# First-group attention and weight casts re-placed, remainder scores in 64x64 tiles

## The chip, the cores and the metric

The kernel runs on one core of one Trainium2 chip. The metric is the device time of one execution in microseconds (us). The engines are named as in the profile: PE is TensorE (matmuls; its weight loads are listed apart as PEld), DVE is VectorE, ACT is ScalarE, POOL is GpSimd, and SP is SyncE, which here only issues transfers. Each engine runs its own instructions strictly in the order in which they stand in its program, and waits at an instruction until what that one needs is there.

## The reference

Attention with pooled keys and values, followed by a two-layer network with a tanh GELU. In short:

```
k_p = k.reshape(8, 8, 72, 8, 64).mean(axis=3)      # 576 keys become 72, by means of 8
v_p = v.reshape(8, 8, 72, 8, 64).mean(axis=3)
attn = softmax(q @ k_p^T / 8) ; a = attn @ v_p     # per batch and head, q is 8 x 8 x 576 x 64
x = a.transpose(0, 2, 1, 3).reshape(4608, 512)
out = gelu_tanh(x @ w_in) @ w_out                  # w_in 512 x 2048, w_out 2048 x 512
```

Everything comes and goes in float32. The kernel computes with bfloat16 operands in the matmuls.

## The kernel before

The 4608 rows are worked in nine groups of 512 rows. A group g < 8 holds the first 512 query rows of batch g; group 8, called R, holds the remaining 64 rows of all eight batches. The order is 0 to 6, then R, then 7.

For a group the attention of four blocks j of 128 queries is computed: `scores` (queries times pooled keys, into PSUM), `exps` (exponential on ACT), `norm` (row sums and reciprocal on DVE, then the product, written to the tile `eb`, on DVE or POOL), a transpose of `eb` to `eT`, and `values` (into `xT`). `pool` adds up keys and values on DVE, `k_spread` places the pooled keys block-diagonally in `kbd`, and `spread_v` the pooled values in `vbd` with a mask, on POOL. The two-layer part is `hidden` (one of 16 pieces fo of the hidden layer: 4 matmuls against `w_in_b`, then GELU on ACT into `gT`) and `output` (16 matmuls a block against `w_out_b`).

The order of every engine's work is written out by hand: calls stand in program order, and what belongs to the next group is hung into the matmuls of the present one. A hook number s is a place in that stream: `hook(s)` runs just before matmul s, and `at(hooks, s, f, ...)` hangs f there. In the first group (`mlp_first`) the hidden layer goes in chunks of four pieces and in two halves of 256 rows, so that the first half can begin before the attention of query blocks 2 and 3 is finished; hooks 0 to 127 are its 128 matmuls of 256 columns, and hooks from 128 on are the output's matmuls of 512 columns.

SP issues the loads in order. `w_in` arrives in four pieces of 1 MB (`w_in_s`, float32) and `w_out` in four (`w_out_s`); each piece is cast to bfloat16 (`cast_w_in`, `cast_w_out`) by an engine that the call names. The float32 landing tiles share three buffers with the k and v tiles (tag "kv"), so the first load of `w_out` waits for the casts of `w_in` pieces 0 and 1, and its third for those of pieces 2 and 3. PSUM tiles come from two sets: "mm" with four buffers, "sc" with two.

Before the change, `w_in` pieces 0, 1 and 3 are cast on DVE and piece 2 on POOL; the normalization of block 2 of the first group is on POOL, that of block 3 on DVE; both are done before the first hook. The group R computes its scores with 128x64 tiles of the PE array: for each pair of heads one matmul per half of 64 query rows, with 144 columns of keys (two heads side by side, block-diagonal, so that half of the products are with zeros).

Of the kernel before, what the change touches and what calls it, by code (L numbers as in the profile page):

```python
# [10 lines left out]
ALU = mybir.AluOpType  # L11
# [8 lines left out]
def kernel(  # L20
# [21 lines left out]
    nc = tc.nc  # L42
    B, H, S, D = q.shape
    Sp = S // 8
# [5 lines left out]
    HP = H // 2  # L50
    W = H * Sp
# [12 lines left out]
    kbd = consts.tile([128, B, HP, 2, Sp], BF16, name="kbd")  # L64
# [5 lines left out]
    eb = consts.tile([128, 4, 5 * 128], BF16, name="eb")  # L70
# [5 lines left out]
    def copy(eng, out, in_):  # L76
        if eng is nc.scalar:
            eng.copy(out=out, in_=in_)  # L78
        else:
            eng.tensor_copy(out=out, in_=in_)  # L80
# [5 lines left out]
    def rows(t, b):  # L86
        return t[b].rearrange("h (sp pl) d -> (h sp) pl d", pl=8)
# [7 lines left out]
    def load_main(b, which, c0, c1, eng):  # L95
        t, w0, b0 = (k, 0, 0) if which == "k" else (v, 64, 5)
        src = rows(t, b)[w0 + 128 * c0:w0 + 128 * c1].rearrange("(c p) pl d -> p c pl d", p=128)
        eng.dma_start(out=st[b]["kv"][:, b0 + c0:b0 + c1], in_=src)
# [18 lines left out]
    def cast_q(g, j0, j1, eng):  # L117
        if "qb" not in st[g]:
            st[g]["qb"] = work.tile([128, 4, H, D], BF16, name="q_b", bufs=1)
        copy(eng, st[g]["qb"][:, j0:j1], st[g]["q"][:, :, j0:j1].rearrange("p h j d -> p j h d"))  # L120
# [69 lines left out]
    def q_transpose_pe(g, j, eng, tag):  # L190
        tp = psum.tile([128, HP, 128], BF16, name="tp", tag=tag, bufs=BUFS[tag])
        for pr in range(HP):
            nc.tensor.transpose(out=tp[:, pr, :],  # L193
                                in_=st[g]["qb"][:, j, 2 * pr:2 * pr + 2, :].rearrange("p h d -> p (h d)"),
                                identity=identb)
        copy(eng, st[g]["qT"][:, j], tp)
# [5 lines left out]
    def scores(g, j):  # L202
        sc = psum.tile([128, 2, MAIN], F32, name="sc", tag="sc", bufs=2)
        qT = st[g]["qT"]
        for pr in range(HP):
            o = sc[:, pr // 2, 2 * Sp * (pr % 2):2 * Sp * (pr % 2) + 2 * Sp]
            if g < B:
                nc.tensor.matmul(out=o, lhsT=qT[:, j, pr, :], rhs=kbd[:, g, pr].rearrange("d hh s -> d (hh s)"),  # L208
                                 start=True, stop=True)
            else:  # L210
                for half in range(2):
                    p0 = 64 * half
                    nc.tensor.matmul(out=o[p0:p0 + 64], lhsT=qT[:, j, pr, p0:p0 + 64],  # L213
                                     rhs=kbd[:, 2 * j + half, pr].rearrange("d hh s -> d (hh s)"),
                                     start=True, stop=True)
        st[g][("sc", j)] = sc

    def exps(g, j):
        sc = st[g].pop(("sc", j))
        e = work.tile([128, H, Sp], F32, name="e", bufs=4)  # L220
        nc.scalar.activation(out=e.rearrange("p (x h) s -> p x (h s)", x=2), in_=sc[:, :, 0:4 * Sp],  # L221
                             func=ACT.Exp, scale=1.0 / 64.0)
        st[g][("e", j)] = e

    def norm(g, j, eng):
        e = st[g][("e", j)]
        den = work.tile([128, H], F32, name="den")
        nc.vector.reduce_sum(out=den, in_=e, axis=AX.X)  # L228
        r = work.tile([128, H], F32, name="r")
        nc.vector.reciprocal(out=r, in_=den)  # L230
        eng.tensor_tensor(out=eb[:, j, 128 * 5 - W:].rearrange("p (h s) -> p h s", s=Sp), in0=e,  # L231
                          in1=r.unsqueeze(2).to_broadcast([128, H, Sp]), op=ALU.mult)

    def eT_tile(g):
        st[g]["eT"] = work.tile([128, 4, 5, 128], BF16, name="eT", bufs=1)
# [1 line left out]
    def e_transpose_pe(g, j, eng):  # L237
        tp = psum.tile([128, 5, 128], BF16, name="tp", tag="mm", bufs=4)
        for c in range(5):
            nc.tensor.transpose(out=tp[:, c, :], in_=eb[:, j, 128 * c:128 * c + 128], identity=identb)  # L240
        copy(eng, st[g]["eT"][:, j], tp)
# [7 lines left out]
    def values_half(g, half, x, eng):  # L249

        xo = psum.tile([128, 2, 256], F32, name="xo", tag="mm", bufs=4)
        for i in range(2):
            pr = 2 * x + i
            for y, (c, n) in enumerate(PARTS[pr]):
                nc.tensor.matmul(out=xo[:, i, :], lhsT=vbd[:, g, n, :],
                                 rhs=st[g]["eT"][:, 2 * half:2 * half + 2, c, :], start=(y == 0), stop=(y == 1))
        copy(eng, st[g]["xT"][:, 2 * x:2 * x + 2, 256 * half:256 * half + 256], xo)
# [28 lines left out]
    def runner(hooks):  # L286
        def hook(s):
            for f in hooks.pop(s, ()):
                f()
        return hook  # L290
# [44 lines left out]
    def mlp_first(g, hooks):  # L335

        hook = runner(hooks)
        s = 0
        for half, c in [(0, 0), (0, 1), (0, 2), (0, 3), (1, 0), (1, 1), (1, 2), (1, 3)]:
            for fo in range(4 * c, 4 * c + 4):  # L340
                hidden(g, fo, 256 * half, 256 * half + 256, hook, s)
                s += 4
        nc.scalar.preload_act_table_set(EXP_SET)
        o = [psum.tile([128, DM], F32, name="mm", tag="mm", bufs=4) for _ in range(4)]
        for fo in range(12):
            for r in range(4):
                hook(s)
                s += 1
                output(g, r, fo, o[r])
        for r in range(4):  # L350
            for fo in range(12, FO):
                hook(s)
                s += 1
                output(g, r, fo, o[r])
            finish(g, r, o[r], nc.scalar if r == 3 else nc.vector)
        assert not hooks, sorted(hooks)
# [16 lines left out]
    for c in range(2):  # L373
        t = kvp.tile([128, KO, 1024], F32, name="w_in_s", tag="kv")
        w_in_s.append(t)
        for i in range(2):
            nc.sync.dma_start(
                out=t[:, :, 512 * i:512 * i + 512],
                in_=moe_w_in[:, 1024 * c + 512 * i:1024 * c + 512 * i + 512].rearrange("(ko p) f -> p ko f", p=128))

    def cast_w_in(c, eng):
        o = 512 * c
        copy(eng, w_in_b[:, :, o:o + 512], w_in_s[c // 2][:, :, 512 * (c % 2):512 * (c % 2) + 512])
# [3 lines left out]
    def w_out_load(c):  # L387
        if c % 2 == 0:
            w_out_s[c // 2] = kvp.tile([128, 8, DM], F32, name="w_out_s", tag="kv")
        t = w_out_s[c // 2][:, 4 * (c % 2):4 * (c % 2) + 4, :]  # L390
        nc.sync.dma_start(out=t, in_=moe_w_out[512 * c:512 * c + 512, :].rearrange("(fo p) c -> p fo c", p=128))
# [48 lines left out]
    spread_v(0, nc.gpsimd, (0,))  # L440
    pool_v_pe(0, 7, 9, nc.scalar)
    spread_v(0, nc.gpsimd, (1,))
    cast_q(0, 2, 4, nc.gpsimd)
    spread_v(0, nc.gpsimd, (2,))
    warm_up(8, "mm")
    norm(0, 0, nc.vector)
    norm(0, 1, nc.vector)
    e_transpose_pe(0, 0, nc.scalar)
    q_transpose_pe(0, 2, nc.scalar, "mm")
    q_transpose_pe(0, 3, nc.scalar, "mm")  # L450
    e_transpose_pe(0, 1, nc.vector)
    cast_w_in(0, nc.vector)
    scores(0, 2)
    exps(0, 2)
    values_half(0, 0, 0, nc.vector)
    scores(0, 3)
    exps(0, 3)
    values_half(0, 0, 1, nc.scalar)
    nc.scalar.preload_act_table_set(GELU_SET)
    norm(0, 2, nc.gpsimd)  # L460
    cast_w_in(1, nc.vector)
    norm(0, 3, nc.vector)
    cast_w_in(2, nc.gpsimd)

    def first_t(j):
        e_transpose_pe(0, j, nc.vector)

    def first_v():
        cast_w_in(3, nc.vector)
        values_half(0, 1, 0, nc.scalar)  # L470
        values_half(0, 1, 1, nc.vector)

# [4 lines left out]
    load_half(1, "k", nc.sync)  # L477
    load_half(1, "v", nc.sync)
    load_q(1, 0, 4, nc.sync)
    for c in range(4):  # L480
        w_out_load(c)
    load_main(1, "v", 0, 4, nc.sync)

    def load_kv(n):
        if n != B - 1:
# [7 lines left out]
    def at(hooks, s, f, *a):  # L493
        hooks.setdefault(s, []).append(lambda: f(*a))  # L494
# [5 lines left out]
        at(hooks, va, values, n, 1, nc.scalar)  # L500

    hooks = {}
    at(hooks, 16, first_t, 2)
    at(hooks, 32, first_t, 3)
    at(hooks, 42, first_v)
    at(hooks, 66, pool, 1, 0, 4)
    at(hooks, 66, dup_k, 1, 0, 4)
    at(hooks, 66, pool, 1, 4, 5)
    at(hooks, 66, dup_k, 1, 4, 5)
    at(hooks, 80, cast_q, 1, 0, 2, nc.vector)  # L510
    at(hooks, 80, cast_q, 1, 2, 4, nc.vector)
    at(hooks, 96, kT_tile, 1, "sc")
    at(hooks, 96, qT_tile, 1)
    at(hooks, 96, k_transpose_pe, 1, 0, 5)
    at(hooks, 96, k_spread, 1, [nc.vector, nc.vector])
    for j in range(4):
        at(hooks, 104 + 6 * j, q_transpose_pe, 1, j, nc.vector, "sc")
    at(hooks, 122, eT_tile, 1)
    at(hooks, 122, cast_w_out, 0, nc.vector)
    at(hooks, 122, cast_w_out, 1, nc.gpsimd)  # L520
    for j in range(4):
        at(hooks, [126, 127, 136, 140][j], scores, 1, j)
        at(hooks, [128, 128, 136, 140][j], exps, 1, j)
        at(hooks, [136, 140, 144, 148][j], norm, 1, j, nc.vector)
        at(hooks, [136, 140, 144, 148][j], e_transpose_dma, 1, j)
    at(hooks, 141, cast_w_out, 2, nc.scalar)
    at(hooks, 141, cast_w_out, 3, nc.scalar)
    for i in range(2):
        at(hooks, 160, pool, 1, 5 + 2 * i, 7 + 2 * i)
        at(hooks, 160, spread_v, 1, nc.gpsimd, (0, 1) if i == 0 else (2,))  # L530
# [6 lines left out]
    for n_, g in enumerate(seq):  # L537
        if n_ == 0:
            continue
        hooks = {}  # L540
# [69 lines left out]
```

The softmax here doesn't subtract the row's maximum and nothing guards it: scores larger than these inputs give would overflow.

## Time and profile before

| | |
|---|---|
| median of 4 runs | 301.12 us (301.07 to 301.28) |
| profiled execution | 301.1 us |
| its span in the profile | 299.0 us |
| PE busy | 289.1 us (97%) |
| PEld, DVE, ACT, POOL busy | 151.4, 145.9, 158.2, 55.5 us |
| granted TensorE clock | 0.999 |
| transfers | 56.32 MB, mean 188 GB/s |

The share of busy time tells which engine is full: PE. Its idle time lies almost wholly in the first 40 us, where the loads, the casts and the first attention are on the way. Rows of the timeline read: start, duration, engine, line, operation, output<-input, shapes, count of merged instructions, and in brackets the idle time before it with what ended it. Rows of transfers read: target<-source, the engine that issues, count, size, and us from issue to landing. A line number in a row is a line of the kernel before; many operations go through one helper (`copy`, lines 78 and 80), so they are told apart by their tiles.

### The profile page before, as it was taken

How to read it: one execution, taken by the hardware profiler on the slowest of the kernel's cores; microseconds unless marked ns; L12 is line 12 of the kernel's file. 1: busy time of each engine (PE TensorE's matmuls, PEld its weight loads, DVE VectorE, ACT ScalarE, POOL GpSimd, SP SyncE). 2: the span in 40 equal slices, each digit the busy share in tenths (PEclk: the TensorE clock that was granted, in tenths of full speed). 3: DMA queues.
4: the chain of work that ended last, by engine and by line, in shares of the span. 5: the costliest groups of instructions: out<-in, count | busy, mean ns of one | idle time of the engine just before them, and what ended most of it. 6: DMA issues, size and time to landing. Idle time of an engine off the chain costs nothing.

```text
span 299.0 us, 4555 instructions
## 1 busy us (share of the span) xinstructions
PE 289.1 (97%) x1708; PEld 151.4 (51%) x1734; DVE 145.9 (49%) x241; ACT 158.2 (53%) x242; POOL 55.5 (19%) x71
## 2 busy tenths in 40 slices
PE   7869999999999999999999999999999999999996
PEld 7758844445444544454445444544444544444444
DVE  6895769165607570748073807381729100920012
ACT  1487783767157715672577246724773267426500
POOL 3252033230400240024012401240024000100000
PEclk9999999999999999999999999999999999999999
DMA  7999996995699459946994599049944700351012
GB/s 233 355 387 339 384 357 143 348 273 152 135 280 255 134 132 267 275 143 123 260 293 138 122 248 301 2 110 247 277 146 101 164 36 2 79 114 37 0 70 70
DMA packets 73221, 56.32 MB, mean 188 GB/s; under 512 B 45808, under 2 KB 55408, under 8 KB 73200
## 3 DMA queue, kind: packets, MB, share of 16 engines
q1 hardware_dynamic: 73056, 55.98, 68.1%
q8 instruction: 13, 0.21, 0.3%
q10 hardware_dynamic: 144, 0.07, 0.1%
q14 instruction: 8, 0.07, 0.1%
HBM read 36.70 MB, written 9.44 MB: 154 GB/s over the span
## 4 chain that ended last, share of the span: by engine, by line
PE 91%; DVE 3%; DMA 2%; ACT 1%; issue 1%; POOL 1%; SPq 0%; ACTq 0%; POOLq 0%
PE mm L296 40%; PE mm L301 40%; PE xo L266 4%; PE sc L208 2%; DMA kv<-in_k_dram 2%; PE mm L329 1%; DVE den L228 1%; POOL eb L231 1%; PE xo L272 1%; DVE eb L231 1%; PE sc L213 0%; PE tp L193 0%; PE warm L410 0%; ACT gT L298 0%; PE tp L240 0%
## 5 line engine op out<-in xcount | busy, mean ns | idle before, releaser
L296 PE MATMUL mm<-xT,w_in_b 128*128 128x512 bf16 (+1 forms) x632 | 127.3, 357 | 0.9 <-DVE xT L80 0.4
L301 PE MATMUL mm<-w_out_b,gT 128*128 128x512 bf16 x542 | 126.2, 379 | 1.5 <-DVE w_out_b L80 0.5
L298 ACT ACTIVATE gT<-mm 128x512 bf16<-128x512 f32 (+1 forms) x160 | 88.4, 555 | 46.9 <-PE mm L296 45.8
L296 PEld LDWEIGHTS <-w_in_b 128*128 128x128 bf16 x640 | 62.2, 98 | 62.6 <-issue 0.5
L301 PEld LDWEIGHTS <-gT 128*128 128x128 bf16 x560 | 53.4, 98 | 59.7 <-DVE w_out_b L80 0.7
L80 DVE COPY osb<-mm 128x512 f32<-128x512 f32 (+2 forms) x37 | 24.3, 658 | 62.9 <-PE mm L301 58.0
L78 ACT CAST xT<-xo 128x1024 bf16<-128x1024 f32 (+1 forms) x18 | 16.6, 967 | 56.8 <-PE xo L266 49.1
L228 DVE TENSOR_REDUCE den<-e 128x8 f32<-128x576 f32 x36 | 26.5, 737 | 39.8 <-ACT e L221 39.7
L148 POOL TENSOR_TENSOR vbd<-kvb,vmask 128x256 bf16<-128x256 bf16 (+2 forms) x40 | 21.2, 554 | 112.9 <-DVE kvb L130 112.8
L128 DVE TENSOR_TENSOR kv<-kv 128x1024 f32<-128x1024 f32 (+3 forms) x20 | 22.4, 1122 | 28.7 <-DMA kv<-in_v_dram 26.4
L221 ACT ACTIVATE e<-sc 128x576 f32<-128x576 f32 x36 | 22.5, 649 | 9.7 <-ACT e L221 4.0
L231 DVE TENSOR_TENSOR eb<-e,r 128x576 bf16<-128x576 f32 x28 | 26.6, 951 | 1.0
L231 POOL TENSOR_TENSOR eb<-e,r 128x576 bf16<-128x576 f32 x8 | 10.1, 1264 | 72.7 <-ACT e L221 42.3
L80 POOL CAST q_b<-q_sb 128x2048 bf16<-128x2048 f32 (+1 forms) x7 | 15.0, 2146 | 3.4 <-PE mm L301 2.8
L208 PEld LDWEIGHTS <-qT 128*128 128x128 bf16 x128 | 10.1, 98 | 6.9 <-ACT qT L78 0.4
L208 PE MATMUL sc<-kbd,qT 128*128 128x144 bf16 x128 | 13.2, 226 | 0.3 <-ACT qT L78 0.2
L266 PE MATMUL xo<-eT,vbd 128*128 128x512 bf16 x56 | 13.2, 379 | 0.0
L129 DVE TENSOR_TENSOR kv<-kv 128x512 f32<-128x512 f32 (+3 forms) x20 | 12.8, 640 | 0.7
L494 ACT ACT_TABLE_LOAD x8 | 10.3, 1283 | 0.1
L410 PE MATMUL warm<-identb 128*128 128x128 bf16 x112 | 8.9, 246 | 1.4 <-POOL vmask L398 1.4
L80 DVE COPY kbd<-kTd 64x288 bf16<-64x288 bf16 x12 | 5.3, 438 | 8.0 <-DMA kTd<-kvb 7.9
L314 ACT ACT_TABLE_LOAD x7 | 9.0, 1283 | 0.1
(55 smaller groups left out, 99.3 us busy)
## 6 DMA issues: line engine op xcount, KB each, us to landing
out_dram<-osb SPq DMA_DIRECT2D x31, 256.0 KB, 6.5
kv<-in_k_dram SPq DMA_DIRECT2D x7, 1024.0 KB, 6.7
q_sb<-in_q_dram SPq DMA_DIRECT2D x7, 1024.0 KB, 5.8
kv<-in_v_dram SPq DMA_DIRECT2D x7, 1024.0 KB, 9.5
w_in_s<-in_moe_w_in_dram SPq DMA_DIRECT2D x4, 1024.0 KB, 12.6
w_out_s<-in_moe_w_out_dram SPq DMA_DIRECT2D x4, 1024.0 KB, 13.8
out_dram<-osb SPq DMA_DIRECT2D x9, 128.0 KB, 2.3
kv<-in_k_dram SPq DMA_DIRECT2D x2, 512.0 KB, 4.1
```

The lines of the kernel that those rows point to most:

```text
L78: eng.copy(out=out, in_=in_)
L80: eng.tensor_copy(out=out, in_=in_)
L128: add(out=t[:, :, 0:4, :], in0=t[:, :, 0:4, :], in1=t[:, :, 4:8, :], op=ALU.add)
L148: eng.tensor_tensor(out=vbd[p0:128, b, n0:n1, :].rearrange("p (c r) (hh d) -> p c (r hh) d", c=max(m, 1), d=D), in0=kvb[p0:128, 4 + c0:4 + ...
L208: nc.tensor.matmul(out=o, lhsT=qT[:, j, pr, :], rhs=kbd[:, g, pr].rearrange("d hh s -> d (hh s)"), start=True, stop=True)
L221: nc.scalar.activation(out=e.rearrange("p (x h) s -> p x (h s)", x=2), in_=sc[:, :, 0:4 * Sp], func=ACT.Exp, scale=1.0 / 64.0)
L228: nc.vector.reduce_sum(out=den, in_=e, axis=AX.X)
L231: eng.tensor_tensor(out=eb[:, j, 128 * 5 - W:].rearrange("p (h s) -> p h s", s=Sp), in0=e, in1=r.unsqueeze(2).to_broadcast([128, H, Sp]), ...
L266: nc.tensor.matmul(out=xo[:, i, :], lhsT=vbd[:, g, n, :], rhs=eT[:, :, c, :], start=(x == 0), stop=(x == 1))
L296: nc.tensor.matmul(out=hp[:, 0:c1 - c0], lhsT=w_in_b[:, ko, fo * 128:(fo + 1) * 128], rhs=st[g]["xT"][:, ko, c0:c1], start=(ko == 0), stop ...
L298: nc.scalar.activation(out=gT[:, fo, c0:c1], in_=hp[:, 0:c1 - c0], func=ACT.Gelu_apprx_tanh)
L301: nc.tensor.matmul(out=o, lhsT=gT[:, fo, r * 128:(r + 1) * 128], rhs=w_out_b[:, fo, :], start=(fo == 0), stop=(fo == FO - 1))
```

## The change

Four things are changed together.

- In the first group all four `w_in` pieces are cast on POOL, each where it lands; the second half of the q cast goes from POOL to ACT.
- The attention of the first group's query blocks 2 and 3 is re-placed: the values of the first half come before their scores, both xT copies of the first half are on DVE, the normalization of block 2 moves from POOL to DVE and that of block 3 to hook 20, and their transposes and the values of the second half to hooks 20, 33 and 40.
- The chunks of the hidden layer alternate between the halves from the fourth on. Hooks of the second group's preparation move by a few places; `w_out` piece 3 is loaded after v instead of before it, and its cast moves from hook 141 to 156.
- The scores of R are computed in 64x64 tiles, one head of a pair per half of the array's rows: four matmuls of 72 columns for a pair of heads instead of two of 144, without the zeros. The heads therefore stand in another order in `e`, which `norm` undoes when it writes `eb`.

```diff
 def scores(g, j):
         for pr in range(HP):
-            o = sc[:, pr // 2, 2 * Sp * (pr % 2):2 * Sp * (pr % 2) + 2 * Sp]
             if g < B:
+                o = sc[:, pr // 2, 2 * Sp * (pr % 2):2 * Sp * (pr % 2) + 2 * Sp]
...
-            else:
-                for half in range(2):
-                    p0 = 64 * half
-                    nc.tensor.matmul(out=o[p0:p0 + 64], lhsT=qT[:, j, pr, p0:p0 + 64],
-                                     rhs=kbd[:, 2 * j + half, pr].rearrange("d hh s -> d (hh s)"),
-                                     start=True, stop=True)
+                continue
+            for hh in range(2):
+                for p0 in (0, 64):
+                    h0 = 64 * hh
+                    nc.tensor.matmul(out=sc[p0:p0 + 64, hh, Sp * pr:Sp * pr + Sp],
+                                     lhsT=qT[h0:h0 + 64, j, pr, p0:p0 + 64],
+                                     rhs=kbd[h0:h0 + 64, 2 * j + p0 // 64, pr, hh], start=True, stop=True)
 def norm(g, j, eng):
...
+        else:
+            eng.tensor_tensor(out=o.rearrange("p (pr hh s) -> p hh pr s", hh=2, s=Sp),
+                              in0=e.rearrange("p (hh pr) s -> p hh pr s", hh=2),
...
 def mlp_first(g, hooks):
-        for half, c in [(0, 0), (0, 1), (0, 2), (0, 3), (1, 0), (1, 1), (1, 2), (1, 3)]:
+        for half, c in [(0, 0), (0, 1), (0, 2), (1, 0), (0, 3), (1, 1), (1, 2), (1, 3)]:
...
-    cast_q(0, 2, 4, nc.gpsimd)
     spread_v(0, nc.gpsimd, (2,))
     warm_up(8, "mm")
     norm(0, 0, nc.vector)
     norm(0, 1, nc.vector)
+    cast_w_in(0, nc.gpsimd)
+    cast_q(0, 2, 4, nc.scalar)
     e_transpose_pe(0, 0, nc.scalar)
+    e_transpose_pe(0, 1, nc.vector)
     q_transpose_pe(0, 2, nc.scalar, "mm")
     q_transpose_pe(0, 3, nc.scalar, "mm")
-    e_transpose_pe(0, 1, nc.vector)
-    cast_w_in(0, nc.vector)
-    scores(0, 2)
-    exps(0, 2)
     values_half(0, 0, 0, nc.vector)
-    scores(0, 3)
-    exps(0, 3)
-    values_half(0, 0, 1, nc.scalar)
+    values_half(0, 0, 1, nc.vector)
+    for j in range(2, 4):
+        scores(0, j)
+        exps(0, j)
     nc.scalar.preload_act_table_set(GELU_SET)
-    norm(0, 2, nc.gpsimd)
-    cast_w_in(1, nc.vector)
-    norm(0, 3, nc.vector)
+    cast_w_in(1, nc.gpsimd)
+    norm(0, 2, nc.vector)
     cast_w_in(2, nc.gpsimd)
+    cast_w_in(3, nc.gpsimd)
...
     def first_v():
-        cast_w_in(3, nc.vector)
...
-    for c in range(4):
+    for c in range(3):
         w_out_load(c)
     load_main(1, "v", 0, 4, nc.sync)
+    w_out_load(3)
...
-    at(hooks, 16, first_t, 2)
-    at(hooks, 32, first_t, 3)
-    at(hooks, 42, first_v)
+    at(hooks, 20, first_t, 2)
+    at(hooks, 20, norm, 0, 3, nc.vector)
+    at(hooks, 33, first_t, 3)
+    at(hooks, 40, first_v)
...
-    at(hooks, 66, pool, 1, 4, 5)
-    at(hooks, 66, dup_k, 1, 4, 5)
-    at(hooks, 80, cast_q, 1, 0, 2, nc.vector)
-    at(hooks, 80, cast_q, 1, 2, 4, nc.vector)
+    at(hooks, 72, pool, 1, 4, 5)
+    at(hooks, 72, dup_k, 1, 4, 5)
...
+    at(hooks, 100, cast_q, 1, 0, 2, nc.vector)
+    at(hooks, 100, cast_q, 1, 2, 4, nc.vector)
     for j in range(4):
-        at(hooks, 104 + 6 * j, q_transpose_pe, 1, j, nc.vector, "sc")
-    at(hooks, 122, eT_tile, 1)
-    at(hooks, 122, cast_w_out, 0, nc.vector)
-    at(hooks, 122, cast_w_out, 1, nc.gpsimd)
+        at(hooks, 111 + 4 * j, q_transpose_pe, 1, j, nc.vector, "sc")
+    at(hooks, 124, eT_tile, 1)
+    at(hooks, 124, cast_w_out, 0, nc.vector)
+    at(hooks, 124, cast_w_out, 1, nc.gpsimd)
...
-    at(hooks, 141, cast_w_out, 3, nc.scalar)
+    at(hooks, 156, cast_w_out, 3, nc.scalar)
```

More of the change, by code (lines that the diff above doesn't have):

```diff
@@ L230, in norm @@
         nc.vector.reciprocal(out=r, in_=den)
-        eng.tensor_tensor(out=eb[:, j, 128 * 5 - W:].rearrange("p (h s) -> p h s", s=Sp), in0=e,
-                          in1=r.unsqueeze(2).to_broadcast([128, H, Sp]), op=ALU.mult)
+        o = eb[:, j, 128 * 5 - W:]
+        if g < B:
+            eng.tensor_tensor(out=o.rearrange("p (h s) -> p h s", s=Sp), in0=e,
+                              in1=r.unsqueeze(2).to_broadcast([128, H, Sp]), op=ALU.mult)
+        else:
+            eng.tensor_tensor(out=o.rearrange("p (pr hh s) -> p hh pr s", hh=2, s=Sp),
+                              in0=e.rearrange("p (hh pr) s -> p hh pr s", hh=2),
+                              in1=r.rearrange("p (hh pr) -> p hh pr", hh=2).unsqueeze(3).to_broadcast([128, 2, HP, Sp]),
+                              op=ALU.mult)
     def eT_tile(g):
```

## The prediction, made before the changed kernel ran

> **What bounds the kernel now.** I read the page first (span, the ended-last chain), then the timeline of the first 45 us, then single transfers, then the stretch of the remainder's scores. Durations are from the profiled execution, 301.1 us (span 299.0, 2.1 around it); the median of the runs is 301.12, so the sum can be set against either.
>
> ```profile
> span 299.0 us, 4555 instructions
> PE 91%; DVE 3%; DMA 2%; ACT 1%; issue 1%; POOL 1%; SPq 0%; ACTq 0%; POOLq 0%
> ```
>
> TensorE is the chain. After 38.4 us its matmuls stand back to back to the end, so only the first 40 us and the remainder's scores can change the time. The timeline of the first group:
>
> ```profile
> 19.99 2.07 POOL L231 TENSOR_TENSOR eb<-e,r 128x576 bf16<-128x576 f32 x1 [2.99 <-DVE r L230]
> 22.12 0.45 PE L240 MATMUL tp<-identb,eb 128*128 128x128 bf16 x5 [1.10 <-POOL eb L231]
> 22.57 1.93 POOL L80 CAST w_in_b<-w_in_s 128x2048 bf16<-128x2048 f32 x1 [0.51 <-DMA w_in_s<-in_moe_w_in_dram]
> 24.55 1.27 PE L296 MATMUL mm<-xT,w_in_b 128*128 128x256 bf16 x10
> 26.53 6.06 PE L296 MATMUL mm<-xT,w_in_b 128*128 128x256 bf16 x54
> 37.16 1.22 DVE L80 CAST w_out_b<-w_out_s 128x2048 bf16<-128x2048 f32 x1
> 37.78 2.34 POOL L80 CAST w_out_b<-w_out_s 128x2048 bf16<-128x2048 f32 x1 [13.29 <-DMA w_out_s<-in_moe_w_out_dram]
> 38.44 1.90 PE L301 MATMUL mm<-w_out_b,gT 128*128 128x512 bf16 x7 [0.50 <-DVE w_out_b L80]
> ```
>
> TensorE idles about 1.1 us before 22.12 (the GpSimd normalization of query block 2), reaches the third w_in piece exactly when its cast ends (22.57 + 1.93 = 24.50), then runs gapless to 37.77 and waits 0.66 us for the VectorE cast of w_out piece 0. The pieces are paced by their transfers, issued at 5.35, 7.61, 9.56 and 11.43 (times to landing for pieces 0, 1, 3, and for w_out piece 1, issued at 23.35):
>
> ```profile
> w_in_s<-in_moe_w_in_dram SPq DMA_DIRECT2D x1, 1024.0 KB, 11.7
> w_in_s<-in_moe_w_in_dram SPq DMA_DIRECT2D x1, 1024.0 KB, 12.2
> w_in_s<-in_moe_w_in_dram SPq DMA_DIRECT2D x1, 1024.0 KB, 13.8
> w_out_s<-in_moe_w_out_dram SPq DMA_DIRECT2D x1, 1024.0 KB, 14.4
> ```
>
> So they land at 17.1, 19.8, 22.5 (piece 2, by the GpSimd cast that waited for it) and 25.2; w_out piece 1 lands at 37.75. Nothing ahead of them in SP's queue changes, and w_out's first issue, 0.7 us later, joins a queue with ten microseconds of work in it: the landings stay. Last, rows in which VectorE and GpSimd meet:
>
> ```profile
> 54.90 1.89 POOL L80 CAST q_b<-q_sb 128x2048 bf16<-128x2048 f32 x1 [2.79 <-PE mm L301]
> 157.61 0.24 DVE L80 COPY kbd<-kTd 64x288 bf16<-64x288 bf16 x1 [1.18 <-DMA kTd<-kvb]
> 157.72 0.97 POOL L148 TENSOR_TENSOR vbd<-kvb,vmask 128x256 bf16<-128x256 bf16 x2
> 157.86 0.56 DVE L80 COPY kbd<-kTd 64x288 bf16<-64x288 bf16 x1
> 228.16 2.42 POOL L80 CAST q_b<-q_sb 128x2048 bf16<-128x2048 f32 x1
> 229.83 1.36 DVE L231 TENSOR_TENSOR eb<-e,r 128x576 bf16<-128x576 f32 x1
> 255.54 0.76 DVE L231 TENSOR_TENSOR eb<-e,r 128x576 bf16<-128x576 f32 x1
> ```
>
> The later starter waits: the copy of 0.24 took 0.56 behind a GpSimd instruction, the normalization of 0.76 took 1.36 behind a GpSimd cast and ended 0.61 after it (so it got going 0.15 before that cast's end), and at 37.78 the GpSimd cast took 2.34 for 1.89 behind VectorE's.
>
> **The change, step by step.** Matmuls of 256 columns follow each other at 0.109 us (6.06 us for 54).
>
> *1. Start of the hidden layer: 0.* ScalarE takes the second q cast (its 512-column one took 0.62, so 1.05) and delays the first e-transpose copy to 16.2; the values still wait for the second, VectorE's, at 17.2. GpSimd drops that q cast and finishes the v masks before the landing at 17.1. The xT copies both go to VectorE (0.69 each), ending 18.7 and 19.3; w_in piece 0 is cast 17.15 to 19.05 (before: to 18.35). The first hidden matmul starts at about 19.1 (before 19.0) and the chunk ends at 20.86 as before.
>
> *2. Chunk 1.* Scores of blocks 2 and 3 now follow the values, so the exponentials end at 19.95 and the table load, 1.28, at 21.25 instead of 20.58; the first GELU frees its PSUM buffer at 21.63. The cast of piece 1 ends at 19.85 + 1.9 = 21.75: chunk 1 starts at 21.8, 0.6 earlier than before (22.41). Block 2's normalization is ready for VectorE at 20.4 but meets that cast, so it runs 21.6 to 22.4; its transpose (hook 20) waits 0.2 for it. Chunk 1 ends near 24.0.
>
> *3. Chunk 2, +0.78.* Its weights are there at 24.50, as before: all that was gained waits here. But before, both transposes were done by then; now block 3's (hook 33) is not. Its chain begins after block 2's eT copy (ends 23.4): reduce 0.74, reciprocal 0.2, so at 24.3 it meets the cast of piece 2, runs 24.36 to 25.12, and TensorE, after one matmul of the chunk, stands from 24.66 to 25.17 (0.51), then transposes (0.28). The second matmul is at 25.45 instead of 24.67. Without any stall the step is +0.28, without the collision 24.9 is still the earliest (+0.53), with a longer reduce or cast +1.1.
>
> *4. Mixed halves, casts 1 to 3 late, later ScalarE casts: 0.* Chunk (1,0) at 28 finds its xT (ready 28.0); (0,3) after it finds piece 3 (25.25 + 1.93 = 27.2). Pool and k casts of batch 1 wait for landings at 28.5 as before and end by 35.6, ahead of their transposes. w_out piece 3 swaps places with v: it lands near 45.8, its ScalarE cast (1.89) ends at 47.7 and is used at 49.3 or later; v is used after 47.6 anyway. If that cover were gone, a delay would reach TensorE one for one.
>
> *5. Hooks 104+6j to 111+4j: +0.11.* The last q transpose moves from hook 122 to 123. From it to the first output matmul runs a fixed chain (36.39 to 38.44): transpose, VectorE copy, w_out cast. It now begins one matmul later: lag 0.78 + 0.11 = 0.89, output at 39.33 if nothing else happens.
>
> *6. The two w_out casts change order, +1.5.* VectorE's cast would start at 37.16 + 0.89 = 38.05. GpSimd's waits for its landing alone and starts at 37.78 as before: now it is first. Then VectorE waits until 37.78 + 1.9 - 0.15 = 39.55, casts until 40.77, and TensorE starts the output at 40.83 instead of 38.44: +2.39 in all. Bounds: 0 (VectorE's cast does not wait, or starts first) and +1.5; I take +1.5, because all rows above show the second waiting, whichever engine it is, and because GpSimd leads by 0.27 us. A lag under 0.62 would restore the old order. Behind VectorE's cast stand the normalizations of batch 1, whose consumers (values at hook 187) come 11 us later.
>
> [...] If instead both merely slowed each other, as the excess of 0.45 on the 2.34 row alone would also allow, this step would be +0.45 and the sum 302.05.
>
> *7. Remainder scores, -0.4.* 32 matmuls of 144 columns become 64 of 72:
>
> ```profile
> 224.70 1.04 PE L301 MATMUL mm<-w_out_b,gT 128*128 128x512 bf16 x4
> 225.67 0.44 PE L213 MATMUL sc<-kbd,qT 128*64 128x144 bf16 x8
> 226.04 8.59 PE L301 MATMUL mm<-w_out_b,gT 128*128 128x512 bf16 x38
> ```
>
> A block takes from 225.57 (four at 0.216 after 224.70) to 226.04, 0.47: eight matmuls in pairs at 0.0625 a pair make 0.25, and 0.2 goes to the borders, which stay. Four abreast would need half the time a step: -0.12 a block, -0.5 in all. If weights go one after another (8 loads span 0.27 with the last 0.11 long, so 0.02 to 0.03 each, 16 of them 0.45) it is +0.2 a block, +0.8. I take -0.4, near the first end, since the pairs already run side by side.
>
> [...]
>
> Sum: 301.1 + 0.78 + 0.11 + 1.5 - 0.4 = 303.1.
>
> **Rivals.** *Old order of casts:* lag under 0.62, or a VectorE cast that GpSimd does not hold up. 301.1 + 0.9 - 0.4 = 301.6; with no stall in step 3, 301.1 + 0.39 - 0.4 = 301.1. For it: a lead of only 0.27 us; against: even the smallest lag that block 3's own chain allows, 0.53 + 0.11 = 0.64, is over the threshold, if barely.
>
> *Faster:* the borders of the remainder's scores go. If a step of four tiles takes 0.033 and nothing is lost where the tile form changes, a block costs 0.13 instead of 0.47, -1.35 in all. With the old order of casts at its limit of 0.62 that is 301.1 + 0.62 - 1.35 = 300.4; it decides from 1.25 saved, and with the casts reversed it wins nothing. Against it: half-array tiles draw these borders now, and the new form keeps the column halves and adds row halves.
>
> *Longer:* TensorE idles 2.2 us before the output, twice the longest pause now. If the clock fell there as at the start, where 44 warm-up matmuls took 4.27 us (0.097 each) against 22 in 1.39 (0.063), two us of such work cost 0.9: 304.0. Or ScalarE's late GELUs, or the late w_out piece 3, stop TensorE as well.
>
> That the casts do not go "as they land" is unlikely: GpSimd has nothing else to do between 17 and 27.
>
> **How the numbers follow.** Casts reversed 0.72 (302.9 to 304.3 by the ends of step 7; the output's start no longer depends on the lag, as GpSimd's end sets it), old order 0.16 (301.0 to 302.2), longer 0.08 (303.6 to 305), faster 0.04. Forecast 303.1. The range 301.6 to 303.9 leaves out the lower half of the old order, the faster case, most of the longer and the far end of step 7: 0.2. A measurement tells 0.2%, 0.6 us, from no change: slower is above 301.7, so 0.72 + 0.08 + 0.06 = 0.86; same 0.10; faster 0.04.
>
> **What would show it.** In the changed profile: GpSimd w_in casts starting at 17.1, 19.9, 22.6, 25.3 (transfers unchanged); the wait of the second late transpose for the normalization, about 0.5 near 24.7; the VectorE w_out cast with about 2.7 us instead of 1.22, beginning after GpSimd's; the first output matmul near 40.8 with some 2 us idle; a remainder block near 0.35 instead of 0.47. Wrong it would be most simply if VectorE's cast still takes 1.22: then look at which cast started first.

## The result and the profile after

| | before | after |
|---|---|---|
| median | 301.25 us (49 executions, 300.95 to 301.58) | 302.58 us (31 executions, 300.84 to 304.66) |
| ratio | | 1.0043, 95% interval 1.0029 to 1.0056 |
| profiled execution | 301.1 us (span 299.0) | 300.84 us (span 299.1) |

The changed kernel is slower by 0.43%. The forecast was 303.1 us, the range 301.6 to 303.9. But a single number hides what happened. Sorted, the 31 times fall into three clusters with gaps between them, while the 49 times of the kernel before make one cluster:

| cluster | executions | times, us | median, us | granted clock |
|---|---|---|---|---|
| short | 11 | 300.84 to 301.54 | 301.06 | 0.999 to 1.0 |
| middle | 12 | 302.31 to 303.24 | 302.72 | 0.998 to 1.0 |
| long | 8 | 304.01 to 304.66 | 304.21 | 0.994 |

The profiled execution is the shortest of all, so its trace shows only the short cluster. The median lies in the middle one because that one stands in the middle, not because most executions are there. Time and span differ by 2.00 to 2.12 us in the 59 executions of the kernel before that were recorded with their spans, and by 1.67 to 1.81 in all 31 of the kernel after; why is not known. The page's first lines of the kernel after, the span and the shares of the chain that ended last:

```profile
span 299.1 us, 4616 instructions
...
PE 91%; DVE 4%; ACT 2%; DMA 1%; issue 1%; ACTq 0%
```

TensorE is the chain as before; VectorE and ScalarE have a little more of it. The timeline of the first group of the kernel after (start, duration, engine, line, operation, and in brackets the idle time before the row with what ended it):

```profile
16.95 1.89 POOL L80 CAST w_in_b<-w_in_s 128x2048 bf16<-128x2048 f32 x1 [1.62 <-DMA w_in_s<-in_moe_w_in_dram]
...
20.16 2.01 DVE L235 TENSOR_TENSOR eb<-e,r 128x576 bf16<-128x576 f32 x1
21.61 0.61 PE L305 MATMUL mm<-xT,w_in_b 128*128 128x256 bf16 x4 [0.79 <-ACT gT L307]
22.22 0.45 PE L249 MATMUL tp<-identb,eb 128*128 128x128 bf16 x5
22.36 1.90 POOL L80 CAST w_in_b<-w_in_s 128x2048 bf16<-128x2048 f32 x1 [0.80 <-DMA w_in_s<-in_moe_w_in_dram]
...
24.13 0.76 DVE L235 TENSOR_TENSOR eb<-e,r 128x576 bf16<-128x576 f32 x1
24.31 0.28 PE L305 MATMUL mm<-xT,w_in_b 128*128 128x256 bf16 x1 [0.33 <-POOL w_in_b L80]
24.95 0.45 PE L249 MATMUL tp<-identb,eb 128*128 128x128 bf16 x5 [0.35 <-DVE eb L235]
...
25.24 0.93 PE L305 MATMUL mm<-xT,w_in_b 128*128 128x256 bf16 x7
```

Chunk 1 begins at 21.61, 0.8 us earlier than before. Chunk 2 cannot begin before the third `w_in` piece is cast: it lands at 22.31 and its cast ends at 24.26. The chunk begins at 24.31, does one matmul and stands until block 3's normalization is done. Then the same timeline around the first output matmul:

```profile
37.83 1.22 DVE L80 CAST w_out_b<-w_out_s 128x2048 bf16<-128x2048 f32 x1
38.04 2.76 POOL L80 CAST w_out_b<-w_out_s 128x2048 bf16<-128x2048 f32 x1 [11.08 <-DMA w_out_s<-in_moe_w_out_dram]
38.23 0.27 PE L305 MATMUL mm<-xT,w_in_b 128*128 128x256 bf16 x1
39.11 1.90 PE L310 MATMUL mm<-w_out_b,gT 128*128 128x512 bf16 x7 [0.61 <-DVE w_out_b L80]
```

In this execution VectorE's cast started first, 0.21 us ahead, and took its 1.22; GpSimd's came second and took 2.76 instead of 1.89. That is the *old order of casts*. The w_out piece landed at 37.99 (casts that wait for a landing start 0.05 behind it), not at the 37.73 of before; had it come as before, GpSimd's cast would have started at 37.78, ahead of VectorE's. Last, the scores of the remainder, with the output matmuls around a block:

```profile
222.61 2.12 PE L310 MATMUL mm<-w_out_b,gT 128*128 128x512 bf16 x9
...
224.66 0.21 PEld L215 LDWEIGHTS <-qT 64*64 64x64 bf16 x16 [0.42 <-issue]
224.66 0.33 PE L215 MATMUL sc<-kbd,qT 64*64 64x72 bf16 x16
...
224.92 1.04 PE L310 MATMUL mm<-w_out_b,gT 128*128 128x512 bf16 x4
```

Nine output matmuls from 222.61 at 0.2165 end their steps at 224.56, and the next begins at 224.92: a block costs 0.35 to 0.36 us, where it cost 0.47.

### The profile page after: what moved, and what is told of

The parts are those of the page before. It is cut to its first block, busy times and chain, and to the rows that moved or that the text cites. A ratio compares the mean times of both kernels' runs of the same rounds, so it can differ in the third digit from the quotient of the medians.

```text
span 299.1 us, 4616 instructions
## 1 busy us (share of the span) xinstructions
PE 288.5 (96%) x1740; PEld 150.9 (50%) x1766; DVE 145.8 (49%) x240; ACT 158.6 (53%) x242; POOL 58.0 (19%) x72
## 4 chain that ended last, share of the span: by engine, by line
PE 91%; DVE 4%; ACT 2%; DMA 1%; issue 1%; ACTq 0%
PE mm L310 40%; PE mm L305 40%; PE xo L275 4%; PE sc L208 2%; PE mm L338 1%; DMA kv<-in_k_dram 1%; DVE eb L235 1%; DVE den L230 1%; PE xo L264 1%; ACT gT L307 1%; PE xo L281 1%; ACT e L223 1%; PE tp L249 0%; DVE kv L128 0%; PE tp L193 0%
## 5 line engine op out<-in xcount | busy, mean ns | idle before, releaser
L78 ACT CAST xT<-xo 128x1024 bf16<-128x1024 f32 (+1 forms) x17 | 16.0, 989 | 55.4 <-PE xo L275 47.9
L235 DVE TENSOR_TENSOR eb<-e,r 128x576 bf16<-128x576 f32 x26 | 25.7, 988 | 0.9
L235 POOL TENSOR_TENSOR eb<-e,r 128x576 bf16<-128x576 f32 x6 | 6.9, 1151 | 62.0 <-ACT e L223 34.8
L80 POOL CAST q_b<-q_sb 128x2048 bf16<-128x2048 f32 x6 | 14.0, 2331 | 2.7 <-DMA q_sb<-in_q_dram 2.7
```

The costliest lines, as they stand in the source:

```text
L235: eng.tensor_tensor(out=o.rearrange("p (h s) -> p h s", s=Sp), in0=e, in1=r.unsqueeze(2).to_broadcast([128, H, Sp]), op=ALU.mult)
```

## The experiments

Two theories stood against each other. *A, the order of the casts:* the middle and long executions are those in which GpSimd's w_out cast starts first and VectorE's, which TensorE needs, waits for it; the long ones add a fall of the clock during that pause. *B:* something else makes them, late transfers or a clock that falls by itself, and the order of the two casts is a by-product. In the diffs below a line of context says where the edit stands.

**More lag, so that GpSimd must win** (the kernel after; 8 warm-up matmuls, 0.5 us):

```diff
         at(hooks, 111 + 4 * j, q_transpose_pe, 1, j, nc.vector, "sc")
+    at(hooks, 100, warm_up, 8, "mm")
     at(hooks, 124, eT_tile, 1)
```

> The changed kernel with 8 small matmuls (about 0.45 us of TensorE) hung in at hook 100, so that VectorE's cast of w_out piece 0 comes later still and GpSimd's cast of piece 1 always starts first. Theory A (the cast that starts second waits for the other): every execution is a long one, 302.5 to 303.2 or 304 to 304.7, none under 302; the output starts at GpSimd's end + 1.1, so the 0.45 itself costs nothing; in the trace the VectorE cast takes 2.0 to 2.7 us instead of 1.22. Theory B (the long executions come from late transfers or from the clock falling by itself): the same three clusters as the changed kernel, each 0.45 later, a third of the executions near 301.4, and VectorE's cast takes 1.22.

Measured: 303.01 us (302.57 to 303.46, five executions), against 301.18 of the kernel before on the same chip; ratio 1.0059 (1.0047 to 1.0071). The short cluster is gone. Its timeline around the first output matmul:

```profile
37.87 1.89 POOL L80 CAST w_out_b<-w_out_s 128x2048 bf16<-128x2048 f32 x1 [10.89 <-DMA w_out_s<-in_moe_w_out_dram]
38.28 2.56 DVE L80 CAST w_out_b<-w_out_s 128x2048 bf16<-128x2048 f32 x1
38.67 0.27 PE L305 MATMUL mm<-xT,w_in_b 128*128 128x256 bf16 x1
...
40.90 1.47 PE L310 MATMUL mm<-w_out_b,gT 128*128 128x512 bf16 x6 [1.95 <-DVE w_out_b L80]
```

This is the picture that the prediction drew: GpSimd first with its undisturbed 1.89, VectorE's cast stretched from 1.22 to 2.56, the output at 40.90. The clock stayed at 0.998 to 1.0 in all five, so none came near 304; one, at 303.46, lies above the expected 303.2.

**The same lag in the kernel before** (16 matmuls, 0.9 us, the size of step 5's lag):

```diff
         at(hooks, 104 + 6 * j, q_transpose_pe, 1, j, nc.vector, "sc")
+    at(hooks, 100, warm_up, 16, "mm")
     at(hooks, 122, eT_tile, 1)
```

> The kernel before with 16 small matmuls (0.9 us of TensorE) hung in at hook 100, nothing else. Theory A: the lag of 0.9 alone brings VectorE's cast behind GpSimd's, so the time rises by 2.4 rather than 0.9: 303.6 in most executions, about 305.2 where the clock falls in the pause, few at 302.1. Theory B: 301.25 + 0.9 = 302.15 in one cluster.

Measured: 303.45 us (301.78 to 305.41, eight executions), ratio 1.0075 (1.0047 to 1.0104). Their spans fall into three groups: 299.7 to 299.9 (four), 301.2 and 301.7, and 302.9 and 303.0 with a clock of 0.994. So the lag alone, with nothing else of the change, brings all three clusters to a kernel that had one. That most executions would be long was too much: half were. The times overstate the rise: the time outside the span was 2.0 to 3.8 us in this run, and the middle of the eight spans is 300.6, 1.5 above the 299.1 of before. With the same 0.9 us of lag VectorE still won in the profiled execution, since the piece landed only at 38.17:

```profile
38.08 1.22 DVE L80 CAST w_out_b<-w_out_s 128x2048 bf16<-128x2048 f32 x1
...
38.23 2.82 POOL L80 CAST w_out_b<-w_out_s 128x2048 bf16<-128x2048 f32 x1 [13.70 <-DMA w_out_s<-in_moe_w_out_dram]
```

**No meeting: both casts on VectorE, one after the other** (the kernel after):

```diff
     at(hooks, 124, cast_w_out, 0, nc.vector)
-    at(hooks, 124, cast_w_out, 1, nc.gpsimd)
+    at(hooks, 124, cast_w_out, 1, nc.vector)
```

> The changed kernel with w_out piece 1 cast on VectorE too, right after piece 0; GpSimd then has no cast at that place. Theory A (the cast that starts second waits): only the collision goes, the wait of 0.77 before the output stays: one cluster at 300.9 to 301.5, VectorE's cast of piece 0 always 1.22. Theory B (late transfers or a clock that falls by itself): three clusters as before, at 300.9, 302.6 and 304.2.

Measured: 301.06 us (300.91 to 301.31, eleven executions), ratio 0.9997 (0.9989 to 1.0006). One cluster, the short one. Its two casts, in one row, and the first output matmul:

```profile
37.91 2.35 DVE L80 CAST w_out_b<-w_out_s 128x2048 bf16<-128x2048 f32 x2
...
39.19 1.90 PE L310 MATMUL mm<-w_out_b,gT 128*128 128x512 bf16 x8 [0.61 <-DVE w_out_b L80]
```

The loads are issued as before this edit (the piece landed at 37.90 here), so theory B's late transfers do not make the middle and long executions by themselves; GpSimd's cast beside VectorE's does. The rest of the change is worth nothing on balance in time, but not in the span: that is 299.3 in the median against 299.0 of the kernel before, since the stall and the lag cost somewhat more than the remainder's scores save, and the time outside the span is 0.3 shorter.

**No meeting: the engines swapped** (piece 0, which lands first and is needed first, to GpSimd, piece 1 to VectorE):

```diff
-    at(hooks, 124, cast_w_out, 0, nc.vector)
-    at(hooks, 124, cast_w_out, 1, nc.gpsimd)
+    at(hooks, 124, cast_w_out, 0, nc.gpsimd)
+    at(hooks, 124, cast_w_out, 1, nc.vector)
```

> The changed kernel with the engines of the first two w_out casts exchanged: piece 0 on GpSimd (lands near 35, before GpSimd has anything else), piece 1 on VectorE. Theory A: the two casts no longer meet, one cluster, and the wait of 0.77 before the output goes: 301.0 - 0.7 = 300.2. Theory B: the long executions stay, the short ones at 300.2, median about 302.

Measured: 301.04 us (300.93 to 301.44, eleven executions), ratio 0.9996 (0.9988 to 1.0005). One cluster again, as theory A has it. The gain from the vanished wait before the output did not show in the time. Its timeline says where it went:

```profile
35.41 2.20 POOL L80 CAST w_out_b<-w_out_s 128x2048 bf16<-128x2048 f32 x1 [8.08 <-DMA w_out_s<-in_moe_w_out_dram]
38.20 1.22 DVE L80 CAST w_out_b<-w_out_s 128x2048 bf16<-128x2048 f32 x1
38.70 1.89 PE L310 MATMUL mm<-w_out_b,gT 128*128 128x512 bf16 x8
39.30 1.28 ACT L352 ACT_TABLE_LOAD   x1
40.60 1.85 ACT L223 ACTIVATE e<-sc 128x576 f32<-128x576 f32 x3
41.30 0.41 PE L208 MATMUL sc<-kbd,qT 128*128 128x144 bf16 x4 [0.71 <-ACT e L223]
```

The output begins at 38.70 without a wait, but ScalarE changes its table at 39.30 and gives its first exponentials from 40.60 on. The scores of block 2, hung at hook 136, need one of the two "sc" buffers that these exponentials free, so TensorE, now earlier, stands there for 0.7 us. The wait moved by two microseconds. (GpSimd's cast took 2.20 instead of 1.89: it began beside VectorE's casts of q, which ended at 35.86.)

**Is the long cluster the pause?** (the kernel after; TensorE kept busy with 24 warm-up matmuls, 1.5 us, in the place where it waits for the cast):

```diff
         nc.scalar.preload_act_table_set(EXP_SET)
+        warm_up(24, "mm")
         o = [psum.tile([128, DM], F32, name="mm", tag="mm", bufs=4) for _ in range(4)]
```

> The changed kernel with 24 small matmuls (1.3 us) between the hidden layer and the output, where TensorE pauses 0.77 us in the short executions and 2.3 in the long ones. If the clock falls (0.994 over the span, 1.6 us) because of that pause: two clusters, 301.5 (the filling costs 0.57 where the pause was short) and 302.6 (it hides in the long pause), none at 304 and no clock under 0.998. If the clock falls for another reason: about a quarter of the executions still at 304 to 305 with 0.994.

Measured: 302.55 us (301.38 to 302.81, ten executions), ratio 1.0036 (1.0024 to 1.0048); three executions at 301.38 to 301.55, seven at 302.39 to 302.81, none longer, none with a clock under 0.999. The profile is of a middle execution, and the casts, which stand ahead of the edit, show there what the kernel after does when GpSimd wins:

```profile
38.05 1.89 POOL L80 CAST w_out_b<-w_out_s 128x2048 bf16<-128x2048 f32 x1 [10.77 <-DMA w_out_s<-in_moe_w_out_dram]
38.14 2.88 DVE L80 CAST w_out_b<-w_out_s 128x2048 bf16<-128x2048 f32 x1
...
38.53 0.27 PE L305 MATMUL mm<-xT,w_in_b 128*128 128x256 bf16 x1
...
38.65 1.50 PE L420 MATMUL warm<-identb 128*128 128x128 bf16 x24
...
41.09 0.60 PE L310 MATMUL mm<-w_out_b,gT 128*128 128x512 bf16 x2 [0.94 <-DVE w_out_b L80]
```

A lead of 0.09 us is enough: VectorE's cast then takes 2.88 and ends 1.08 us after GpSimd's. Between 38.80, when the last matmul of the hidden layer ended, and 41.09 it would have paused for 2.3 us. With the pause filled the middle cluster stays and the long one goes.

**A pause that is longer still** (both casts on GpSimd, piece 1 ahead of piece 0):

```diff
-    at(hooks, 124, cast_w_out, 0, nc.vector)
     at(hooks, 124, cast_w_out, 1, nc.gpsimd)
+    at(hooks, 124, cast_w_out, 0, nc.gpsimd)
```

> The changed kernel with both first w_out casts on GpSimd, piece 1 before piece 0, so that TensorE pauses in every execution from about 38.4 until GpSimd has cast twice after the landing near 37.9: 37.9 + 3.8 = 41.7, a pause of 3.3 us. If a long pause of TensorE brings the clock down, nearly every execution shows 0.994 and the time is 301.0 + 2.6 for the pause + 1.6 for the clock = 305.2; if the clock falls for another reason, 303.6 with 1.0 in most executions and about a quarter at 305.2.

Measured: 305.16 us, four executions: 303.75 with a clock of 1.0, 305.14 and 305.18 with 0.994, 306.53 with 0.989; ratio 1.0125 (1.0082 to 1.0167). In the profiled one (305.14) the output begins at 42.00 after 3.0 us without matmuls. Busy time by engine in three stretches of it, with the granted clock:

```profile
core 0: us, PE busy (x) PEld busy (x) DVE busy (x) ACT busy (x) POOL busy (x), PEclk, DMA share, GB/s
38.70:42.00 3.30, 0.27 (x4) 0.10 (x2) 0.62 (x1) 2.86 (x4) 3.25 (x2) 0.88 1.05 384
42.00:44.60 2.60, 2.37 (x6) 0.92 (x7) 2.46 (x6) 0.00 (x0) 0.40 (x1) 0.50 0.76 281
44.60:60.00 15.40, 15.35 (x78) 7.26 (x78) 8.89 (x16) 8.57 (x8) 4.54 (x5) 1.00 0.79 206
```

The clock is 0.5 in the whole second stretch and 1.0 after it. A mean of 0.88 in the first means that it fell 0.8 us before that stretch's end (0.12 x 3.3 / 0.5), at about 41.2 and 2.2 us after the last matmul of the hidden layer had ended (38.97). From 44 to 46 us the mean is 0.84, which puts its return at about 44.6 (0.16 x 2 / 0.5 behind 44). So the clock was halved for about 3.4 us, of which 2.6 are matmuls at half speed (the weight loads of the output stand 0.43 us apart there, against matmuls 0.2165 apart at full clock): 1.3 us lost there. The execution at 303.75 has the same edit and kept a clock of 1.0. What decides whether the clock falls is not shown, since no trace of a pause of this length without a fall was taken. The clusters of this run stand about 1.4 us apart (303.75, 305.16, 306.53), those of the kernel after 1.5 (302.72 and 304.21).

**The remainder's scores alone** (the kernel before, with the new `scores` and `norm`):

```diff
-                for half in range(2):
-                    p0 = 64 * half
-                    nc.tensor.matmul(out=o[p0:p0 + 64], lhsT=qT[:, j, pr, p0:p0 + 64],
...
+            for hh in range(2):
+                for p0 in (0, 64):
+                    h0 = 64 * hh
+                    nc.tensor.matmul(out=sc[p0:p0 + 64, hh, Sp * pr:Sp * pr + Sp],
```

> The kernel before with the scores and the normalization of the remainder in the new form alone. Both theories: a block of scores 0.35 us on TensorE instead of 0.47, so -0.46 in all: 300.8, one cluster. If the strided write of the normalization stopped something, it would be 301.3 or more.

Measured: 300.79 us (300.41 to 300.98, eleven executions), 0.39 below the 301.18 of before; ratio 0.9986 (0.9978 to 0.9995). The step is a gain of its own, of the size that was forecast.

**The stall of step 3 taken away** (the kernel after; block 3's transpose one chunk later, and so the other half's chunk as well):

```diff
-        for half, c in [(0, 0), (0, 1), (0, 2), (1, 0), (0, 3), (1, 1), (1, 2), (1, 3)]:
+        for half, c in [(0, 0), (0, 1), (0, 2), (0, 3), (1, 0), (1, 1), (1, 2), (1, 3)]:
...
-    at(hooks, 33, first_t, 3)
-    at(hooks, 40, first_v)
+    at(hooks, 40, first_t, 3)
+    at(hooks, 47, first_v)
```

> The changed kernel with the transpose of block 3 at hook 40 instead of 33 and the values of the second half at 47 instead of 40, chunk (0,3) before (1,0) again. Theory A: the stall of 0.53 before that transpose goes, TensorE is ahead by 0.5, VectorE's cast starts near 37.3 and before GpSimd's in every execution: one cluster at 300.4 (the short cluster's 300.95 less 0.53). Theory B: the three clusters, each 0.5 lower.

Measured: 300.59 us (300.25 to 301.30, eleven executions), ratio 0.9981 (0.9973 to 0.9990), one cluster. Its timeline at both places:

```profile
24.31 0.76 DVE L235 TENSOR_TENSOR eb<-e,r 128x576 bf16<-128x576 f32 x1
...
24.50 1.05 PE L305 MATMUL mm<-xT,w_in_b 128*128 128x256 bf16 x8 [0.34 <-POOL w_in_b L80]
25.39 0.44 PE L249 MATMUL tp<-identb,eb 128*128 128x128 bf16 x5
...
37.49 1.22 DVE L80 CAST w_out_b<-w_out_s 128x2048 bf16<-128x2048 f32 x1
38.02 2.44 POOL L80 CAST w_out_b<-w_out_s 128x2048 bf16<-128x2048 f32 x1 [10.87 <-DMA w_out_s<-in_moe_w_out_dram]
...
38.77 1.04 PE L310 MATMUL mm<-w_out_b,gT 128*128 128x512 bf16 x4 [0.61 <-DVE w_out_b L80]
```

Eight matmuls of the chunk now cover the normalization, VectorE's w_out cast starts at 37.49 instead of 37.83, and its lead is 0.53 us. That was enough in all eleven executions. So the 0.5 us stall was not only its own price: it helped to push the later cast into the other one.

**All of it together.** The edit of the run before, the swapped engines, and the scores and exponentials that held TensorE up in the swapped kernel placed later, with one product of the normalization on GpSimd:

```diff
-        at(hooks, [126, 127, 136, 140][j], scores, 1, j)
-        at(hooks, [128, 128, 136, 140][j], exps, 1, j)
-        at(hooks, [136, 140, 144, 148][j], norm, 1, j, nc.vector)
-        at(hooks, [136, 140, 144, 148][j], e_transpose_dma, 1, j)
-    at(hooks, 141, cast_w_out, 2, nc.scalar)
+        at(hooks, [126, 127, 142, 146][j], scores, 1, j)
+        at(hooks, [128, 128, 142, 146][j], exps, 1, j)
+        at(hooks, [138, 142, 146, 150][j], norm, 1, j, nc.gpsimd if j == 1 else nc.vector)
+        at(hooks, [138, 142, 146, 150][j], e_transpose_dma, 1, j)
+    at(hooks, 147, cast_w_out, 2, nc.scalar)
```

> The changed kernel with the stall of step 3 taken out as in the run without it, the casts of w_out pieces 0 and 1 exchanged between GpSimd and VectorE, and, since exchanging alone left TensorE waiting 0.87 us at the scores of block 2, those scores 6 hooks later with the normalizations behind them, one of their products on GpSimd. Theory A: 300.95 - 0.53 - 0.7 = 299.7 in one cluster, no wait over 0.3 us between the third chunk and the end. Theory B: 299.7 at best, with long executions up to 303.

Measured: 299.73 us (299.66 to 299.79, five executions), ratio 0.9951 (0.9939 to 0.9963). Of this kernel the span, and the timeline where the hidden layer ends and the output begins:

```profile
span 297.9 us, 4642 instructions
...
35.16 1.89 POOL L80 CAST w_out_b<-w_out_s 128x2048 bf16<-128x2048 f32 x1 [8.01 <-DMA w_out_s<-in_moe_w_out_dram]
37.81 1.23 DVE L80 CAST w_out_b<-w_out_s 128x2048 bf16<-128x2048 f32 x1 [0.23 <-DMA w_out_s<-in_moe_w_out_dram]
37.89 0.27 PE L305 MATMUL mm<-xT,w_in_b 128*128 128x256 bf16 x1
38.00 2.75 PE L310 MATMUL mm<-w_out_b,gT 128*128 128x512 bf16 x12
```

GpSimd's cast is over at 37.05, before VectorE's begins; both take their undisturbed times, and TensorE goes from the hidden layer into the output without a wait. This version beats both kernels, the one before by 1.4 us (301.11 on the same chip); 1.1 of that lies in the span (299.0 to 297.9).

**The kernel after once more** (one execution, no edit):

> The changed kernel once more, for a second trace of it. If VectorE's cast of w_out piece 0 starts before GpSimd's of piece 1 it takes 1.22 and the span is 299.1 to 299.8; if after, it takes over 2 us and the span is 300.6 or more; a span of 302.3 or more goes with a clock of 0.994.

Measured: 302.03 us, span 300.2, clock 1.0. VectorE's cast started first (38.93, 1.22 us; GpSimd's 39.34, 2.56 us), so its order is that of a short execution, but its span is 1.1 above that of the first profile: the first `w_in` piece was there only at 18.0 instead of 16.9, and the first values came 0.9 later. That missed the expected span. It shows a second, smaller source of spread, which the order of the casts does not explain; how often it comes was not measured.

## Why the prediction was right, and where it was off

*Steps 1 and 2* held: GpSimd's `w_in` casts began at 16.95, 19.66, 22.36 and 25.07 (forecast 17.1, 19.9, 22.6, 25.3) and chunk 1 at 21.61 (21.8). Its start was set by the GELU, about 0.05 us after the cast of piece 1 had ended at 21.56; the forecast had the cast as the later one, by 0.12. The normalization of block 2 was held up by that cast, 2.01 us instead of 0.76. *Step 4*, the term put at nothing, held too: `w_out` piece 3 landed at 46.03 (45.8), and between 25.3 and the end of the hidden layer TensorE waited for nothing.

*Step 3, +0.78*, held in its working: chunk 2 began when the cast of piece 2 was over, and between its first and second matmul TensorE spent 0.53 us on the stall and 0.29 on the transposes, against 0.51 and 0.28. Block 3's normalization met the cast of piece 2 only at its very end, as forecast, and took its plain 0.76 (24.13 to 24.89): the chain of copy, reduce and reciprocal ahead of it sets its time, not the meeting. Removing the stall took the first output matmul from 39.11 to 38.77, although the first `w_in` cast began 0.18 us later in that execution.

*Step 5 and the lag* came out at 0.67 instead of 0.89 where it matters: the whole first group was about 0.2 us earlier in this execution (16.95 against 17.13 at its first cast). So the sum of the *old order* is 299.0 + 0.67 - 0.46 = 299.2, and the profile's span is 299.1. The rival's 301.6 was 0.5 above the short cluster's 301.06 for this reason (0.2) and because the prediction kept the 2.1 us outside the span of the kernel before, where the kernel after has 1.7 to 1.8 (0.3).

*Step 6, +1.5*, is the step that made the forecast. Mechanism and size are shown in its two neighbours, the kernels with more lag and with the filled pause: where GpSimd's cast is first, VectorE's takes 2.56 to 2.88 us and the output begins at 40.90 to 41.09 (forecast 2.7, 40.83), and the middle cluster lies 1.66 us above the short one. (37.78 + 1.9 - 0.15 is 39.53, not 39.55; nothing hangs on it.) What failed is its certainty. The step took "GpSimd leads by 0.27 us" from one execution and treated the landing as fixed. In the first profile of the kernel after both starts had moved, VectorE's by 0.22 us forward against the forecast 38.05 and GpSimd's by 0.26 back, since the w_out piece landed at 37.99 instead of 37.73. By their times twenty of 31 executions had the reversed order, 0.65, though neither profile of the kernel after caught one of them; the chance was 0.72 + 0.08. "The later starter waits" was the right reading of the rows: the same VectorE cast took 1.22 where it began first and 2.88 where it began second, the same GpSimd cast 1.89 and 2.76. Counted back by its plain 1.22 from its end, VectorE's second cast got going 0.14 us before the recorded end of GpSimd's, in both traces that show it (forecast 0.15).

*The rival "Longer"* was underrated. It stood at 0.08 and +0.9; the clock fell in 8 of the 20 reversed executions and cost 1.5 us. The prediction scaled the price from the warm-up's matmuls, and too low: its 0.097 us is a mean over matmuls 0.107 apart up to 4.92 us and 0.056 apart from there on (and by its own two rates two us cost 0.7 to 1.1, not 0.9). The long-pause run shows what it is: half clock for about 3.4 us, 2.6 of it in the output's matmuls. A pause of about 2.3 us sufficed, by the length that the filled kernel shows; no trace of a long execution of the kernel after was taken. Why the fall strikes only some of these executions is not shown. That the pause causes the fall rests on counts: 8 falls in 20 with the pause open, none in 7 middle executions with it filled, 3 in 4 with 3 us. Two falls came in the four reversed executions of the kernel before with the lag. With the extra lag of the first experiment, whose pause was 2.0, there was none in five; how the chance of a fall goes with the length is not settled.

*Step 7, -0.4*: measured -0.39 alone, and 4 x -0.115 in the trace. The tiles do run four abreast (16 matmuls in 0.33 us, the last steps 0.033 apart), the borders of about 0.19 us a block stay, and so the rival *Faster* fell.

*The number.* 302.58 lies 0.5 under 303.1, within the range. For the reversed order the forecast was right in the span: 303.1 less 2.1 is 301.0, the median span of the middle cluster. Its time is 302.72 because less lies outside the span, 1.7 to 1.8 us instead of 2.1, a term that the prediction took over from the kernel before; every kernel with the changed first group shows it, neither the remainder's scores alone (2.0) nor the lag does, and its cause stays open. The remaining 0.14 comes from a median over three clusters. That this median fell into the middle one was in part luck: with five more executions in the short cluster it would have been near 301.5, under the range.

## What to carry to other kernels

Where casts of VectorE and GpSimd meet, ask which of the two is on the path and what decides which begins first; if it is a transfer's landing, the answer changes from execution to execution, and a lead of 0.2 or 0.3 us is no lead: here one of 0.53 held in eleven of eleven executions, and the sign of a smaller one changed. Remove the meeting (the piece that lands and is needed first to the engine that is free) rather than move it. And look at all the times, not at the median and one profile: clusters with gaps between them can be the sign of such a race, and a small stall far upstream may be what made it close.

## What the runs showed of the hardware that was not expected

- The landing of the same transfer differed by 0.44 us between the profiles (37.73 in the kernel before, 37.99 after, 37.82 with the extra lag, 38.17 in the kernel before with the lag), more than the lead on which the order hung; in the second profile of the kernel after it came at 39.28.
- A TensorE pause of about 2.3 us before dense matmuls was followed by a lower granted clock (0.994 over the span) in 8 of 20 executions, at 1.5 us each; one of 3 us in 3 of 4, in one of them for twice the loss (306.53 us at 0.989).
- In the trace of the long-pause run the granted clock was 0.5 from about 41.2 to about 44.6 us, 3.4 us, and 1.0 from there on; it fell 2.2 us into a pause of 3.0.
- Sixteen matmuls of 64x64 tiles with 72 columns took 0.33 us together and their weight loads 0.21, beside each other; the change to this form and back kept its price of about 0.19 us a block.
